# A kernel whose ring of small buffers is moved down by 480 bytes in SBUF

## The chip, the cores and the metric

The kernel runs on one core of a Trainium2 chip. The metric is device time in microseconds (us), the median of the runs shown; lower is better. One more execution was recorded by the hardware profiler, and all rows below come from that one.

## What is computed

Three stages in a row, all in float32. First attention over 4 batches and 8 heads of 768 positions with 64 elements per head: each query sees the 31 keys within 15 positions of it, and one summary (maximum of keys, mean of values) of each block of 32 positions. Its output is read as 3,072 tokens of 512 elements. Second, a wide layer; third, a mixture of 8 experts with 4 slots each:

```python
# wide layer, x is [3072, 512], w_in [512, 2048], w_out [2048, 512]
h = x @ w_in
g = h * np.cos(h)
x2 = g @ w_out
# mixture
logits = x2 @ phi                      # [3072, 32]
d = softmax(logits, axis=0); slot_input = d.T @ x2
slot_out = [np.maximum(slot_input[e] @ w1[e], 0) @ w2[e] for e in range(8)]
out = softmax(logits, axis=1) @ slot_out
```

## The kernel before, in words

**The wide layer.** The tokens are taken in six batches of 512. In each batch the inner width of 2,048 is taken in 16 slots of 128, so there are 96 slots. To keep float32 accuracy with single-pass matmuls, each operand is split into a rounded high part and a remainder (fp32r tiles): the tokens into `xh` and `xl` (lines 536 and 540), a slot's weights into `wih`, `wil`, `woh`, `wol` (lines 553 and 560), the slot's result `g` into `gh` and `gl` (lines 622 and 631). A product then takes three matmuls: high by high, high by remainder, remainder by high.

**The first product** of a slot (`mm1_hi`, `mm1_lo`; lines 580, 581, 588) is 12 matmuls into one PSUM bank, each with 128x128 stationary weights and a moving operand of 512 columns:

```python
nc.tensor.matmul(h, hi[:, c], xh[s // NF][:, t, :], start=t == 0, stop=False)   # 580
nc.tensor.matmul(h, hi[:, c], xl[s // NF][:, t, :], start=False, stop=False)    # 581
nc.tensor.matmul(h, lo[:, c], xh[s // NF][:, t, :], start=False, stop=t == 3)   # 588
```

The stationary operand (second argument) is a slice of 128 columns, 512 bytes, of `wih` or `wil`; the moving one is a whole row of 2,048 bytes of `xh` or `xl`.

**The second product** (`mm2_hi`, `mm2_lo`; lines 666, 667, 675) is 12 matmuls into four banks, the stationary operand a slice of `gh` or `gl`, the moving one the whole of `woh` or `wol`:

```python
nc.tensor.matmul(acc[t], gh[:, c], hi, start=f == 0, stop=False)                # 666
nc.tensor.matmul(acc[t], gh[:, c], lo, start=False, stop=False)                 # 667
nc.tensor.matmul(acc[t], gl[:, c], hi, start=False, stop=f == NF - 1)           # 675
```

In the last batch (`mm2_last`; lines 652, 653, 655) the two change places: `woh` and `wol` are stationary, `gh` and `gl` move. In every stream of these matmuls each one needs weights of its own to be loaded, and the load for the next one runs beside the current one.

**Between the matmuls** of a slot, VectorE and ScalarE compute `g` (lines 600, 604, 608, 618), ScalarE rounds (lines 553, 622) and GpSimd takes the remainders (lines 560, 631). Between slots stand pieces of attention for later batches (scores L382, transposes L467, values L502) and of the mixture (transposes L712, logits L726, sums L837). After the last batch the experts run (L1172, L1218) and the outputs are combined (L1253); their weights `ex` come by DMA into buffers as these are released.

**Order.** The order on every engine up to slot 80 is written out by name in a long string (`ORDER`), the rest follows the order of the code. Addresses play no part in it.

**Places in SBUF.** Pools are laid from address 0 upward, those with `side="right"` from the upper end downward. The pool `ring` holds the eleven small kinds of tile named above except `xh` and `xl`; every one of them is 2,048 bytes per partition, so all of them begin at the same remainder by 2,048. `xh` and `xl` lie in the pool `xres`; their rows are 2,048 bytes too. In the built kernel:

| tiles | pool | address in a partition | remainder by 2,048 |
|---|---|---|---|
| `xh`, `xl` (rows of 2,048 bytes) | xres | 69,120 to 101,888 | 1,536 |
| `gh`, `gl` | ring | 196,576 to 208,864 | 2,016 |
| `wih`, `woh`, `wol` | ring | 208,864 to 221,152 | 2,016 |
| `a`, `wil` | ring | 221,152 to 229,344 | 2,016 |
| weights `w` as loaded | wres | 3,584 to 69,120 | 1,536 |

When the wide layer is done, the pool `tail` takes the place of `ring`: seven tiles of expert weights (`ex`), which later hold four of the twelve output tiles, and one tile `cT0`. Ten tiles of the first attention batches (`aT`) lie in the ring as well.

Of the kernel before, what the change touches and what calls it, by code (L numbers as in the profile page):

```python
# [10 lines left out]
F32 = mybir.dt.float32  # L11
# [60 lines left out]
def body(ctx: ExitStack, tc: tile.TileContext, q0, qk, kT, vT, vn, vx, w, phi, ex, cst, out):  # L72
# [7 lines left out]
    ps_acc = ctx.enter_context(tc.tile_pool(name="ps_acc", bufs=1, space=PSUM))  # L80
    ps_h = ctx.enter_context(tc.tile_pool(name="ps_h", bufs=2, space=PSUM))
    ps_m = ctx.enter_context(tc.tile_pool(name="ps_m", bufs=2, space=PSUM))
    ring_cm = tc.tile_pool(name="ring", bufs=2, side="right", reuse_waits="tile")
    ring = ring_cm.__enter__()
    att_cm = tc.tile_pool(name="att", bufs=2, reuse_waits="tile")
# [1265 lines left out]
```

## Time and profile before

| | |
|---|---|
| median of 3 runs | 719.12 us (718.82 to 720.0) |
| profiled execution, its own time | 720.67 us |
| its span, first to last instruction | 718.9 us |
| TensorE (PE) busy | 701.7 us, 98% of the span |
| PE's weight loads (PEld), beside the matmuls | 545.8 us |
| VectorE (DVE) / ScalarE (ACT) / GpSimd (POOL) busy | 440.9 / 409.7 / 412.5 us |
| mean granted clock of TensorE | 0.996 |

The span holds nearly all of the profiled execution's time (1.8 us lie around it). Matmuls overlap: the record of one runs on while the next has begun, so the distance from one start to the next tells what a matmul costs, and the length of its record does not.

### The profile page before, as it was taken

What the parts mean: (1) busy time and instruction counts of PE and PEld (TensorE: products, weight loads), DVE (VectorE), ACT (ScalarE), POOL (GpSimd) and SP (SyncE); (2) the same over time, 40 slices, a digit from 0 to 9 for tenths busy, and PEclk for the clock granted to TensorE, in tenths of its full rate; (3) what the DMA queues carried; (4) which work ended last, traced back from release to release, by engine and by line L of the source; (5) the groups of instructions that cost most, each with busy time, mean ns of one, the idle gap of its engine ahead of it and who ended that gap; (6) DMA issues with size and microseconds to landing.
All of it is one profiled execution on the core that took longest, in us unless ns stands there. A gap on an engine that the chain in (4) does not pass through costs nothing.

```text
span 718.9 us, 12964 instructions
## 1 busy us (share of the span) xinstructions
PE 701.7 (98%) x5092; PEld 545.8 (76%) x5092; DVE 440.9 (61%) x680; ACT 409.7 (57%) x772; POOL 412.5 (57%) x310
## 2 busy tenths in 40 slices
PE   8999999999999999999999999999999999999994
PEld 6678777888787788878887787887787887787453
DVE  6799988784665856855756765665763335434323
ACT  5999997563754654744654844644745446434122
POOL 1776867765566564665754675754667665752000
PEclk9999999999999999999999999999999999999998
DMA  9998866210413302202102203101002922327998
GB/s 334 421 345 288 317 207 245 77 58 0 133 36 139 105 1 78 98 0 105 53 1 72 83 1 107 46 1 46 28 1 84 407 105 79 116 89 273 409 375 291
DMA packets 34861, 101.64 MB, mean 141 GB/s; under 512 B 3440, under 2 KB 13936, under 8 KB 32752
## 3 DMA queue, kind: packets, MB, share of 16 engines
q1 hardware_dynamic: 34800, 100.81, 38.4%
q8 instruction: 40, 0.66, 0.4%
q14 instruction: 21, 0.17, 0.1%
HBM read 92.54 MB, written 6.29 MB: 137 GB/s over the span
## 4 chain that ended last, share of the span: by engine, by line
PE 89%; DMA 4%; ACT 3%; DVE 1%; issue 1%; SPq 0%; DVEq 0%
PE h L580 13%; PE h L581 12%; PE h L588 12%; PE acc L666 10%; PE acc L675 10%; PE acc L667 10%; DMA raw<-in_w_dram 4%; PE av L502 3%; PE sc L382 2%; PE tr L467 2%; PE acc L652 2%; PE acc L653 2%; PE acc L655 2%; PE yp L1218 2%; PE hp L1172 2%; PE xt L712 1%
## 5 line engine op out<-in xcount | busy, mean ns | idle before, releaser
L631 POOL TENSOR_TENSOR gl<-a,gh 128x512 fp32r<-128x512 f32 x96 | 131.0, 1366 | 115.2 <-ACT gh L622 70.0
L560 POOL TENSOR_TENSOR wol<-w,woh 128x512 fp32r<-128x512 f32 x96 | 127.7, 1333 | 82.3 <-ACT woh L553 75.7
L580 PE MATMUL h<-xh,wih 128*128 128x512 f32 x384 | 155.3, 404 | 2.3 <-DVE a L618 1.4
L581 PE MATMUL h<-xl,wih 128*128 128x512 f32 x384 | 151.9, 395 | 0.2 <-DVE xl L540 0.2
L600 DVE TENSOR_SCALAR a<-h 128x512 f32<-128x512 f32 x96 | 66.0, 687 | 126.0 <-PE h L588 84.9
L608 ACT ACTIVATE a<-a,halfpi 128x512 f32<-128x512 f32 x96 | 69.4, 723 | 105.1 <-DVE a L604 104.7
L666 PE MATMUL acc<-woh,gh 128*128 128x512 f32 x320 | 127.3, 398 | 0.0
L667 PE MATMUL acc<-wol,gh 128*128 128x512 f32 x320 | 125.4, 392 | 0.0
L560 POOL TENSOR_TENSOR wil<-w,wih 128x512 fp32r<-128x512 f32 x81 | 108.5, 1345 | 16.9 <-ACT wih L553 8.9
L588 PE MATMUL h<-xh,wil 128*128 128x512 f32 x384 | 105.1, 398 | 0.0
L618 DVE TENSOR_TENSOR a<-h,a 128x512 f32<-128x512 f32 x96 | 65.7, 687 | 43.3 <-ACT a L608 43.0
L580 PEld LDWEIGHTS h<-xh,wih 128*128 128x128 f32 x384 | 72.1, 188 | 22.6 <-DVE a L618 2.3
L675 PE MATMUL acc<-woh,gl 128*128 128x512 f32 x320 | 88.3, 397 | 0.0
L588 PEld LDWEIGHTS h<-xh,wil 128*128 128x128 f32 x384 | 71.0, 188 | 17.6 <-POOL wol L560 0.8
L581 PEld LDWEIGHTS h<-xl,wih 128*128 128x128 f32 x384 | 72.1, 188 | 16.0 <-DVE xl L540 0.5
L553 ACT CAST woh<-w 128x512 fp32r<-128x512 f32 x96 | 59.4, 619 | 40.3 <-PE acc L675 34.3
L553 ACT CAST wih<-w 128x512 fp32r<-128x512 f32 x96 | 59.1, 619 | 28.5 <-PE h L581 18.4
L622 ACT CAST gh<-a 128x512 fp32r<-128x512 f32 x96 | 58.9, 616 | 26.8 <-PE acc L667 19.2
L666 PEld LDWEIGHTS acc<-woh,gh 128*128 128x128 f32 x320 | 60.1, 188 | 14.8 <-issue 1.5
L667 PEld LDWEIGHTS acc<-wol,gh 128*128 128x128 f32 x320 | 60.2, 188 | 12.9
L675 PEld LDWEIGHTS acc<-woh,gl 128*128 128x128 f32 x320 | 58.7, 188 | 12.8 <-issue 0.3
L604 DVE SCALAR_TENSOR_TENSOR a<-a,h 128x512 f32<-128x512 f32 x96 | 65.5, 683 | 2.3
(155 smaller groups left out, 946.6 us busy)
## 6 DMA issues: line engine op xcount, KB each, us to landing
ex<-in_ex_dram SPq DMA_DIRECT2D x64, 512.0 KB
raw<-in_w_dram SPq DMA_DIRECT2D x16, 1024.0 KB
qk<-in_qk_dram SPq DMA_DIRECT2D x20, 736.0 KB
v<-in_vx_dram SPq DMA_DIRECT2D x24, 512.0 KB
kr<-in_kT_dram SPq DMA_DIRECT2D x16, 384.0 KB
out_dram<-o SPq DMA_DIRECT2D x12, 512.0 KB
vr<-in_vT_dram SPq DMA_DIRECT2D x12, 384.0 KB
v<-vs SPq DMA_DIRECT2D x40, 48.0 KB
```

Source lines behind the costliest of these rows:

```text
L553: nc.scalar.copy(hi, W[f][:, part, :])
L560: (eng or nc.gpsimd).tensor_tensor(out=lo, in0=W[f][:, part, :], in1=hi, op=ALU.subtract)
L580: nc.tensor.matmul(h, hi[:, c], xh[s // NF][:, t, :], start=t == 0, stop=False)
L581: nc.tensor.matmul(h, hi[:, c], xl[s // NF][:, t, :], start=False, stop=False)
L588: nc.tensor.matmul(h, lo[:, c], xh[s // NF][:, t, :], start=False, stop=t == 3)
L600: nc.vector.tensor_scalar(out=a, in0=h, scalar1=0.25, scalar2=MAGIC, op0=ALU.add, op1=ALU.add)
L608: turn_dve["sin"] = nc.scalar.activation(a, a, AF.Sin, bias=halfpi, scale=-TWO_PI)
L618: nc.vector.tensor_tensor(out=a, in0=h, in1=a, op=ALU.mult)
L631: nc.gpsimd.tensor_tensor(out=gl, in0=a, in1=gh, op=ALU.subtract)
L666: nc.tensor.matmul(acc[t], gh[:, c], hi, start=f == 0, stop=False)
L667: nc.tensor.matmul(acc[t], gh[:, c], lo, start=False, stop=False)
L675: nc.tensor.matmul(acc[t], gl[:, c], hi, start=False, stop=f == NF - 1)
```

## The change

One line is added, ahead of the pool `ring`. It reserves a tile of 120 float32 elements, 480 bytes per partition, at the upper end of SBUF. Nothing reads or writes it. No instruction is added, removed or moved on any engine.

```diff
     ps_m = ctx.enter_context(tc.tile_pool(name="ps_m", bufs=2, space=PSUM))
+    ctx.enter_context(tc.tile_pool(name="edge", bufs=1, side="right")).tile([128, 120], F32, name="edge")
     ring_cm = tc.tile_pool(name="ring", bufs=2, side="right", reuse_waits="tile")
```

All tiles of `ring`, and later of `tail`, lie 480 bytes lower: `gh` at 196,096 in place of 196,576, and so on, with remainder 1,536 in place of 2,016. All other tiles stay where they were.

## Rows read from the trace of the kernel before

**Rows 1.** Windows: busy us (instructions) of each engine, granted clock, DMA.
```profile
34.00:100.00 66.00, 63.86 (x446) 49.76 (x445) 60.03 (x88) 64.32 (x143) 46.17 (x27) 1.00 0.81 294
100.00:200.00 100.00, 100.00 (x697) 80.28 (x696) 72.48 (x103) 62.74 (x102) 67.67 (x49) 1.00 0.35 120
...
400.00:500.00 100.00, 99.57 (x638) 79.33 (x630) 62.62 (x93) 54.49 (x93) 62.42 (x50) 1.00 0.15 49
500.00:600.00 100.00, 100.00 (x616) 80.04 (x615) 50.71 (x83) 50.79 (x88) 66.77 (x52) 1.00 0.32 123
600.00:659.00 59.00, 59.00 (x263) 46.56 (x265) 23.97 (x39) 28.68 (x48) 35.04 (x28) 1.00 0.35 122
659.00:719.00 60.00, 48.84 (x551) 28.12 (x551) 20.30 (x46) 15.57 (x33) 0.73 (x1) 0.95 0.95 354
```

**Rows 2.** Waits, whole span: engine and line <- releaser: us, times, longest.
```profile
DVE a L600 <- PE h L588: 84.9, 40, 5.1
...
ACT woh L553 <- PE acc L675: 34.3, 24, 5.2
...
PE h L580 <- DVE a L618: 1.4, 2, 1.0
```

**Rows 3.** PE timeline, 139 to 150 us: start, length, line, operation, count.
```profile
139.49 2.03 PE L588 MATMUL h<-xh,wil 128*128 128x512 f32 x8
141.36 1.09 PE L675 MATMUL acc<-woh,gl 128*128 128x512 f32 x4
142.29 0.39 PE L666 MATMUL acc<-woh,gh 128*128 128x512 f32 x1
...
144.12 1.07 PE L675 MATMUL acc<-woh,gl 128*128 128x512 f32 x4
145.02 0.39 PE L666 MATMUL acc<-woh,gh 128*128 128x512 f32 x1
...
146.84 0.40 PE L580 MATMUL h<-xh,wih 128*128 128x512 f32 x1
...
149.64 0.39 PE L580 MATMUL h<-xh,wih 128*128 128x512 f32 x1
```

**Rows 4.** Lengths of the matmuls' records, whole span: minimum, median, maximum in ns.
```profile
L588 PE MATMUL h<-xh,wil x384: 388/396/505, 36.9 to 650.3; 128*128 128x512 f32 x192
L675 PE MATMUL acc<-woh,gl x320: 387/390/504, 52.6 to 570.9; 128*128 128x512 f32 x160
L655 PE MATMUL acc<-gl,woh x64: 389/389/434, 575.7 to 658.6; 128*128 128x512 f32 x64
```

**Rows 5.** Groups of PE, 100 to 659 us: line, shape, count; busy us, mean ns.
```profile
L580 PE MATMUL h<-xh,wih 128*128 128x512 f32 x340 | 137.0, 403 | 0.4 <-DVE a L618 0.4
L581 PE MATMUL h<-xl,wih 128*128 128x512 f32 x340 | 134.4, 395 | 0.0
L666 PE MATMUL acc<-woh,gh 128*128 128x512 f32 x288 | 114.6, 398 | 0.0
...
L588 PE MATMUL h<-xh,wil 128*128 128x512 f32 x343 | 94.1, 398 | 0.0
...
L652 PE MATMUL acc<-gh,woh 128*128 128x512 f32 x64 | 25.5, 399 | 0.0
```

**Rows 6.** Groups of PE over the whole span: the work between the streams.
```profile
L467 PE MATMUL tr<-ident,S 128*120 128x128 f32 x192 | 27.8, 275 | 0.1
...
L502 PE MATMUL av<-aT,v 120*64 120x64 f32 x640 | 23.0, 225 | 0.0
L382 PE MATMUL sc<-qk 64*64 64x120 f32 x640 | 21.0, 269 | 0.0
...
L712 PE MATMUL xt<-ident,x 128*128 128x128 f32 x80 | 11.7, 274 | 0.0
```

**Rows 7.** Two lines of GpSimd: minimum, median, maximum ns of one.
```profile
L631 POOL TENSOR_TENSOR gl<-a,gh x96: 1270/1297/2167, 45.0 to 655.5; 128x512 fp32r<-128x512 f32 x96
```
```profile
L560 POOL TENSOR_TENSOR wol<-w,woh x96: 1267/1295/2225, 28.7 to 654.3; 128x512 fp32r<-128x512 f32 x96
```

**Rows 8.** Experts' matmuls: moving tiles outside the ring, then inside: minimum, median, maximum ns.
```profile
L1218 PE MATMUL yp<-ex,hT x32: 379/379/379, 683.4 to 684.9; 128*32 128x256 f32 x32
```
```profile
L1218 PE MATMUL yp<-ex,hT x32: 379/379/379, 685.1 to 686.6; 128*32 128x256 f32 x32
```

## The prediction

> **What bounds the kernel now.** I read the windows by stage first. [...] Then the waits: VectorE waits 84.9 us in all for line 588 and ScalarE 34.3 us for line 675, while the longest entry of TensorE itself is 1.4 us in two waits [rows 2]. So in the wide layer the others wait for TensorE, and TensorE for nobody. What a matmul costs there, from its start to the next one's, is what the time is made of. Between 34 and 100 us it is less clear: ScalarE is busy for 64.32 of 66 us and TensorE for 63.86, so either may set the pace. After 659 us the experts run, with the DMA engines at a share of 0.95.
>
> Then the PE timeline, where the reader is to take differences of starts [rows 3]. Twelve matmuls of the first product, from 146.84 to 149.64 us, take 2.80 us: 233.3 ns each. Eight of line 588, from 139.49 to 141.36, take 1.87: 234 ns. The first twelve of the second product behind them, to 144.12, take 2.76: 230 ns. The next twelve, to 146.84, take 2.72: 226.7 ns. So there are two levels, although all are 128x128 by 128x512 in the same type, at the same clock. The second product begins high and settles at 226.7 ns; the first stays at about 233.3. This is no matter of one stretch: the median record of line 588 is 396 ns long, of line 675 390, and of line 655 in the last batch 389 [rows 4]; where matmuls follow each other closely, the record's length moves with the distance.
>
> What differs between the two? Not the shape, nor the reuse of weights: lines 580 and 581 load one slice twice and move two tiles, and so do 666 and 667. Not the bank of the output: 666 and 667 write one bank twice, line 675 a new one each time, and both are among the twelve at 226.7. Not the slice of the weights: both products step through a tile by 512 bytes. Not which tile stands still: in the last batch `wo` and `g` change places, and line 655 still has the low level. What is left is where the operands lie. In the second product both begin at remainder 2,016 by 2,048. In the first the moving rows begin at 1,536 and the weights at 2,016; by 512, to which the slices step, that is a difference of 32 bytes against none. Also, `xh` and `xl` lie far below the ring. The trace holds these differences only together, so which of them matters can't be read from it.
>
> **The change part by part.** *What it adds in work:* nothing. Every engine has the same instructions in the same order with the same waits, and the reserved tile is never touched: 0 us.
>
> *The first product.* After the change the moving rows and the weights both begin at 1,536, a difference of none, as the second product has it now. If the difference is what costs, these matmuls fall to 226.7 ns once settled. From 100 to 659 us there are 340 + 340 + 343 = 1,023 of them [rows 5], at 233.3 - 226.7 = 6.6 ns: 6.75 us.
>
> *The second product.* Both operands move together, so their difference stays none. Its first dozen behind the first product costs 230 and not 226.7 [rows 3]. If that is the rest of another rhythm, it goes when the first product has the same one. There are 3 x 288 + 3 x 64 = 1,056 [rows 5], nearly all within a dozen of such a switch: 3.3 ns each, 3.5 us.
>
> *What stays.* The streams are interrupted, and I assume that each new beginning costs a dozen at 230: 12 x 3.3 = 0.04 us. The pieces between: 192/4 = 48 blocks of transposes, 640/32 = 20 of values and 20 of scores, 80/4 = 20 of the mixture's transposes [rows 6], 108 in all, some before 100 us: about 100, or 4.0 us.
>
> *Sum:* 6.75 + 3.5 - 4.0 = 6.2 us. Its ends: if the first product only comes to the 230 that the second has behind a switch, and the second gains nothing, 1,023 x 3.3 = 3.4 us. If no beginning costs anything, 10.2 us. I take 6.2 because the rows show both the settled level and the dozen before it.
>
> *Stage 34 to 100 us:* I count nothing, with ScalarE busy for 97% of it [rows 1]; if TensorE sets the pace there, the other 129 and 96 matmuls would give 1.2 us more.
>
> *The other engines' reads and writes of the ring.* GpSimd's line 631 has all three operands at 2,016 and a median of 1,297 ns; line 560 reads one at 1,536 and has 1,295 [rows 7]. Equal remainders cost no more than 2 ns there, so I price the move at 0; the 96 instructions of each line at 2 ns would be 0.4 us on an engine that is busy for two thirds of the time.
>
> *What is late next.* A slot of about 7 us would shorten by 0.08 us, and VectorE alone waits nearly 0.9 us a slot for line 588 [rows 2]. So TensorE stays the bound. If that cover failed, the gain would be lost slot by slot, down to nothing.
>
> *The experts' stage.* Their weights are loaded as buffers come free, which TensorE paces; before 659 us the DMA share is 0.35 [rows 1], so loads that start earlier meet no crowd, and the stage moves forward whole. Without that, only the last batch's part, 59 of 559 us, would be lost: 0.7 us. Seven weight tiles, four output tiles and `cT0` also move; their matmuls are in the part that I price at 0 (below).
>
> **The profiled execution against the median.** It took 720.67 us, above all three runs, of which the median is 719.12. With 6.2 us less its span would be 712.7 and its own time 714.5; the median becomes 719.12 - 6.2 = 712.9 us.
>
> **Rivals.**
>
> *Nothing changes: 719.1 us.* The two levels may come from where the tiles lie in the large, 69 to 102 thousand against 197 and more, or from something that I haven't named; 480 bytes don't touch that. For it: in the experts' matmuls, moving tiles outside the ring at 1,536 and tiles in it at 2,016 give records of 379 ns alike [rows 8], and GpSimd doesn't care either. Against it: those matmuls load only 32 columns of weights, so little is read beside the moving operand, and the two levels are there all the same in the streams. [...]
>
> *Slower: 722.6 us.* The start of the moving operand decides alone: at 1,536 a stream doesn't settle, at 2,016 it does. Then the first product stays as it is, and the second, whose `woh` and `wol` now begin at 1,536, loses its low level: 1,056 x (233.3 - 230) = 3.5 us. For it: in the streams, 1,536 goes with the high level and 2,016 with the low one without exception. Against it: [rows 8] show no such effect of the moving start alone, and an even start of both operands is no evident handicap. It decides if 666, 667 and 675 no longer come to 226.7.
>
> *A part of the gain: 715.7 us.* The first product comes to 230 only, as in the lower end above. This is within the forecast's own range.
>
> **How the numbers follow.** The forecast (both products settle) has 0.57, with its own range of 708.5 (the 10.2 us and a little of the early stage) to 715.7. No change has 0.27, the slower rival 0.16. About 0.2%, 1.4 us, is what a measurement of this kernel can tell from no change. So faster 0.57, same 0.27, slower 0.16. The range from 708.5 to 720.4 takes in the forecast and no change, and leaves out the slower rival.
>
> **What the changed profile would show.** Right: in the PE timeline twelve matmuls of lines 580 and 581 (one line further down in the new file) in 2.72 to 2.76 us and not 2.80, the median record of line 588 at about 390 ns and not 396, the first dozen of the second product behind the first at 2.72; TensorE still busy all through the wide layer; GpSimd's medians within a few ns of 1,295. If lines 580, 581 and 588 still step by 233.3, the first term was wrong; if 666, 667 and 675 rise to 233, the slower rival holds; if the steps fall and the time doesn't, the cover of the other engines was too thin.

## The result, and the profile after

The changed kernel takes **712.1 us** (median of four runs, 711.56 to 712.95), against 719.56 us (718.82 to 720.1) for the kernel before on the same chip: a ratio of 0.9898, with a 95% interval of 0.9883 to 0.9913. The prediction was 712.9 us, "faster" with a chance of 0.57, and a range of 708.5 to 720.4. The profiled execution took 712.95 us with a span of 711.2; before, it was 720.67 with 718.9. So the spans differ by 7.7 us, the medians by 7.5.

The PE timeline of the changed kernel, at the place of [rows 3] (start us, length us, engine, line, operation, count; every line below the inserted one stands one further down, so 580, 581, 588, 666, 667, 675 are now 581, 582, 589, 667, 668, 676):

```profile
138.09 1.98 PE L589 MATMUL h<-xh,wil 128*128 128x512 f32 x8
139.90 1.07 PE L676 MATMUL acc<-woh,gl 128*128 128x512 f32 x4
...
142.62 1.07 PE L676 MATMUL acc<-woh,gl 128*128 128x512 f32 x4
...
145.34 0.39 PE L581 MATMUL h<-xh,wih 128*128 128x512 f32 x1
...
148.06 0.39 PE L581 MATMUL h<-xh,wih 128*128 128x512 f32 x1
```

Take the differences of the starts. Eight of line 589: 138.09 to 139.90, 1.81 us and no longer 1.87. The dozen of the second product behind them: 2.72 and no longer 2.76. The next dozen 2.72, as before. The dozen of the first product, 145.34 to 148.06: 2.72 and no longer 2.80. All of them now step by about 226.7 ns. The work is the same, instruction for instruction.

The lengths of the records answer [rows 4] (minimum, median, maximum in ns):

```profile
L589 PE MATMUL h<-xh,wil x384: 387/389/504, 37.3 to 642.6; 128*128 128x512 f32 x192
...
L676 PE MATMUL acc<-woh,gl x320: 388/389/504, 53.0 to 564.6; 128*128 128x512 f32 x160
...
L656 PE MATMUL acc<-gl,woh x64: 388/389/441, 569.3 to 650.9; 128*128 128x512 f32 x64
```

The median of line 588 was 396; as line 589 it is 389, that of all the others. The windows answer [rows 1] (stretch and its length, then busy us and instructions of PE, its weight loads, DVE, ACT and POOL, granted clock, DMA share, GB/s):

```profile
34.00:100.00 66.00, 64.58 (x460) 51.05 (x457) 60.08 (x88) 65.78 (x145) 47.03 (x28) 1.00 0.80 293
100.00:200.00 100.00, 100.00 (x702) 81.21 (x701) 73.14 (x105) 62.76 (x103) 67.78 (x49) 1.00 0.34 121
...
500.00:600.00 100.00, 100.00 (x569) 81.44 (x567) 52.06 (x87) 52.49 (x93) 69.28 (x54) 1.00 0.31 118
...
652.00:712.00 60.00, 48.12 (x531) 27.54 (x527) 20.27 (x45) 14.98 (x32) 0.73 (x1) 0.95 0.93 352
```

TensorE is still busy through the wide layer at the same granted clock of 1.00. What became shorter is the time from one start to the next, not idle time. The busy times show this badly, since a stretch that was full stays full. The last window is placed 7 us earlier than its counterpart, and its numbers are nearly the same: the experts' stage came forward whole. And the waits, which answer [rows 2] (us in all, times, longest):

```profile
DVE a L601 <- PE h L589: 85.9, 43, 5.0
...
ACT woh L554 <- PE acc L676: 33.2, 24, 5.2
...
PE h L581 <- DVE a L619: 1.8, 3, 1.1
```

VectorE and ScalarE still wait for TensorE, nearly as long as before; TensorE's own longest entry went from 1.4 to 1.8 us. The bound has not moved.

A timeline shows one place. For the whole span I worked out, from the starts of all matmuls in each trace, the mean distance from each matmul of a product to the next matmul of the wide layer, where that follows directly and less than 300 ns later (some 1,050 such distances in the first product and 1,060 in the second). It went from 233.2 to 228.4 ns in the first product and from 229.9 to 228.0 in the second. Each product has 1,152 matmuls: 1,152 x 4.8 = 5.5 us and 1,152 x 1.9 = 2.2 us, 7.7 together if every matmul is counted. That this is just the difference of the spans is in part luck: 0.9 us of that difference is there by 100 us already, where the two traces differ in their clock too (see "The early stage" below). The account from 100 us on is the one to trust: 6.8 us.

### The profile page after: what moved, and what is told of

The parts are those of the page before. It is cut to its first block, busy times and chain, and to the rows that moved or that the text cites. A ratio compares the mean times of both kernels' runs of the same rounds, so it can differ in the third digit from the quotient of the medians.

```text
span 711.2 us, 12964 instructions
## 1 busy us (share of the span) xinstructions
PE 694.8 (98%) x5092; PEld 547.2 (77%) x5092; DVE 440.1 (62%) x680; ACT 409.6 (58%) x772; POOL 411.9 (58%) x310
## 4 chain that ended last, share of the span: by engine, by line
PE 90%; DVE 4%; ACT 3%; issue 1%; DVEq 0%
PE h L581 12%; PE h L582 12%; PE h L589 12%; PE acc L667 10%; PE acc L676 10%; PE acc L668 10%; PE tr L468 3%; PE av L503 3%; PE sc L383 2%; PE acc L653 2%; PE acc L656 2%; PE acc L654 2%; PE yp L1219 2%; PE hp L1173 2%; PE xt L713 1%; PE sp L838 1%
## 5 line engine op out<-in xcount | busy, mean ns | idle before, releaser
L581 PE MATMUL h<-xh,wih 128*128 128x512 f32 x384 | 153.5, 400 | 1.8 <-DVE a L619 1.8
L582 PE MATMUL h<-xl,wih 128*128 128x512 f32 x384 | 150.2, 391 | 0.1
L589 PE MATMUL h<-xh,wil 128*128 128x512 f32 x384 | 103.2, 394 | 0.0
```

## The experiments

The change moves one thing and thereby several: the ring's absolute start, its start against that of `xh` and `xl`, the ring's place, and the bytes left free. My theory was that the *difference* between the start of the moving operand and that of the weights decides. In what follows "difference" is the start of the moving operand minus that of the weights, reduced to 0 to 255 by taking away multiples of 256 (that 256 is the right number came out only in the course of the runs). Before, it was 32 in the first product (1,536 - 2,016 = -480) and 0 in the second. All experiments that change the tile `edge` alone keep the second product's difference at 0.

**Experiment 1: a ring moved by 32 bytes only.** The changed kernel, with 32 free bytes and not 480, which makes the difference 64:

```diff
-    ....tile([128, 120], F32, name="edge")
+    ....tile([128, 8], F32, name="edge")
```

> The ring lies 32 bytes lower than before, not 480: its tiles begin at 1,984 by 2,048, xh and xl stay at 1,536. The difference of moving and stationary starts is then none by 64 bytes, but 64 by 512 and 448 by 2,048. Theory A (the difference by 64 sets the step of a matmul): both products settle at 226.7 ns, the whole gain of the change, median about 712. Theory B (the difference counts by 512 or by 2,048): the first product stays near 233.3 ns, the median at 717 to 719.5.

Measured: 716.47 us, ratio 0.9957 (0.994 to 0.9974); mean distances 230.5 and 229.8 ns in the first and the second product. This is a part of the gain, and neither theory had it. The PE timeline of this run, at the same place:

```profile
145.36 0.40 PE L581 MATMUL h<-xh,wih 128*128 128x512 f32 x1
...
148.12 0.39 PE L581 MATMUL h<-xh,wih 128*128 128x512 f32 x1
```

The dozen takes 2.76 us, between 2.72 and 2.80. So the pattern is not one of equal or unequal remainder by 64: a difference of 64 is better than 32 and worse than 0.

**Experiment 2: move the other operand.** The kernel before, but with 480 free bytes at the lower end, ahead of the pool of `xh` and `xl`. Now `xh` and `xl` begin at 2,016 as well, where the tiles of the ring have always begun:

```diff
+    ctx.enter_context(tc.tile_pool(name="edge", bufs=1)).tile([128, 120], F32, name="edge")
```

> The ring stays where it was (2,016) and the 480 bytes are left free below xh and xl, which then begin at 2,016 too; the tiles between them and the ring move up with them. Differences are none, but every start lies 32 bytes off a multiple of 64. Theory A (only the difference counts): both products settle at 226.7 ns, median about 712. Theory C (starts at a multiple of 64 are what is good): no gain, 719, or, if 2,016 is bad for a moving operand, slower.

Measured: 712.2 us, ratio 0.99 (0.9883 to 0.9918); 228.4 and 228.0 ns, the numbers of the changed kernel. Its PE timeline:

```profile
139.66 1.07 PE L676 MATMUL acc<-woh,gl 128*128 128x512 f32 x4
...
142.38 1.07 PE L676 MATMUL acc<-woh,gl 128*128 128x512 f32 x4
...
145.10 0.39 PE L581 MATMUL h<-xh,wih 128*128 128x512 f32 x1
...
147.82 0.39 PE L581 MATMUL h<-xh,wih 128*128 128x512 f32 x1
```

Each dozen takes 2.72 us. So the ring's absolute start doesn't matter, nor does its place: here it lies where it lay before (the tiles between `xl` and the ring are 480 bytes higher). What is common to this kernel and the changed one is the equal start.

**Experiment 3: nearly as many free bytes, but no equal start.** 448 bytes, which puts the ring at 1,568 and the difference at 224 (-32):

```diff
-    ....tile([128, 120], F32, name="edge")
+    ....tile([128, 112], F32, name="edge")
```

> The ring lies 448 bytes lower than before, its tiles begin at 1,568 by 2,048, nearly where the change puts them, but 32 bytes off xh and xl again. Theory A and theory C: the first product steps by 233 ns as before, the second by 228 to 230, median about 719. If the free space or the rough place of the ring brings the gain: about 712.

Measured: 718.64 us, ratio 0.9994 (0.9972 to 1.0015); 233.2 and 229.0 ns. Its PE timeline:

```profile
145.78 0.40 PE L581 MATMUL h<-xh,wih 128*128 128x512 f32 x1
...
148.58 0.40 PE L581 MATMUL h<-xh,wih 128*128 128x512 f32 x1
```

The dozen takes 2.80 us, as before the change. No gain is shown, though the ring was moved nearly as far. The first product has the same 233.2 as before, 32 bytes on the other side.

**Experiment 4: equal starts in the first product, 32 bytes apart in the second.** The changed kernel, with a small tile in the ring behind one of the buffers, which puts `gh` and `gl` at 1,504 while `wih`, `wil`, `woh` and `wol` stay at 1,536:

```diff
         aT = pool.tile([KC, 512], F32, name=f"aT{g}_{j}", tag=tag, bufs=n)
+        if g == 2 and j == 1:
+            ring.tile([128, 8], F32, name="gap", tag="gap", bufs=1)
```

> The changed kernel with 32 bytes more, between gh, gl and the other tiles of the ring: gh and gl begin at 1,504, the rest at 1,536. The first product keeps equal starts, the second (stationary gh or gl, moving woh or wol) is set 32 bytes apart. Theory A: the first product stays at 227 to 228 ns, the second goes from 228.0 to 233, 1,152 x 5.2 ns = 6.0 us, and the first begins out of step behind it: median 717 to 719. A theory in which the moving start alone counts (woh, wol, xh, xl are all at 1,536 as in the changed kernel): 712.

Measured: 717.56 us, ratio 0.9979 (0.9968 to 0.9989). The first product is at 229.0 ns, the second at 232.9. Its PE timeline (here the lines are two further down again, 583, 591, 669, 678):

```profile
137.88 1.98 PE L591 MATMUL h<-xh,wil 128*128 128x512 f32 x8
139.71 1.09 PE L678 MATMUL acc<-woh,gl 128*128 128x512 f32 x4
...
142.50 1.09 PE L678 MATMUL acc<-woh,gl 128*128 128x512 f32 x4
...
145.30 0.39 PE L583 MATMUL h<-xh,wih 128*128 128x512 f32 x1
...
148.02 0.39 PE L583 MATMUL h<-xh,wih 128*128 128x512 f32 x1
```

The two products have changed roles: the dozens of the second take 2.79 and 2.80 us, that of the first 2.72. The records agree (minimum, median, maximum in ns):

```profile
L591 PE MATMUL h<-xh,wil x384: 387/389/504, 36.6 to 647.3; 128*128 128x512 f32 x192
...
L678 PE MATMUL acc<-woh,gl x320: 388/394/502, 52.3 to 568.1; 128*128 128x512 f32 x160
```

So nothing about the first product itself (its tiles' place, its outputs, its order) gave it the high level; the same level can be given to the second. It also speaks against the rival by which the moving start alone decides: in the second product of this kernel, the moving `woh` and `wol` of batches before the last begin at 1,536, as `woh` and `wol` do in the changed kernel, and yet the level is the high one.

**Experiments 5 to 7: how far the pattern repeats.** The first run had left open which number the difference is to be taken by. Three paddings: 96 bytes (difference 128), 224 (-256, so 0 by 256, but not by 512 or 2,048) and 992 (512, so 0 by 512, but not by 2,048):

```diff
-    ....tile([128, 120], F32, name="edge")
+    ....tile([128, 24], F32, name="edge")     # experiment 5
+    ....tile([128, 56], F32, name="edge")     # experiment 6
+    ....tile([128, 248], F32, name="edge")    # experiment 7
```

> The ring begins at 1,920 by 2,048, xh and xl at 1,536: a difference of 128 by 512 in the first product, none in the second. With 32 bytes apart the first product steps by 233.2 ns, with 64 by 230.5, with none by 228.4. Theory A1 (the pattern repeats every 128 bytes): 228.4 ns and a median of 712. Theory A2 (it repeats every 256 or 512 bytes only): the first product between 229 and 234 ns, a median of 714 to 719.

> The ring begins at 1,792 by 2,048: a difference of 256 by 512 in the first product, none in the second. Theory A1 (repeats every 128) and a pattern of 256: 228.4 ns, a median of 712. A pattern of 512: between 229 and 234 ns, 714 to 719.

> The ring begins at 1,024 by 2,048, 512 away from xh and xl, so the starts agree by 512 and not by 2,048, the remainder that the change names. Since the weights are slices that step by 512 bytes, every form of the theory of differences says that this is as good as the change: 228.4 ns in both products, a median of 712. If the remainder by 2,048 or by 1,024 counts: 714 to 719.

Measured: with 96 bytes 717.79 us, ratio 0.9973 (0.9953 to 0.9993), 232.4 and 229.1 ns; with 224 bytes 713.14 us, 0.9899 (0.9865 to 0.9933), 228.55 and 228.05 ns; with 992 bytes 711.81 us, 0.9887 (0.9837 to 0.9937), 228.3 and 228.0 ns. The records of line 589 in the run with 96, the one with 224 and the one with 992:

```profile
L589 PE MATMUL h<-xh,wil x384: 387/393/505, 36.6 to 647.1; 128*128 128x512 f32 x192
```
```profile
L589 PE MATMUL h<-xh,wil x384: 387/389/628, 37.5 to 643.1; 128*128 128x512 f32 x192
```
```profile
L589 PE MATMUL h<-xh,wil x384: 387/389/504, 35.6 to 640.9; 128*128 128x512 f32 x192
```

Differences of -256, 0 and 512 give the whole gain, 128 gives little of it. So it is enough that the two starts agree by 256 bytes; the 2,048 in the change's description is more than is needed, and any of 224, 480 and 992 free bytes would have done. The intervals of the four versions with equal starts overlap, so none of them is shown to be better than the change.

**Experiments 8 to 10: the points between.** 64, 128 and 160 free bytes, differences of 96, 160 and 192:

```diff
-    ....tile([128, 120], F32, name="edge")
+    ....tile([128, 16], F32, name="edge")     # experiment 8
+    ....tile([128, 32], F32, name="edge")     # experiment 9
+    ....tile([128, 40], F32, name="edge")     # experiment 10
```

> Difference of 96 by 256 in the first product, none in the second. So far by 256: none 228.4 to 228.6 ns, 32 and 224 both 233.2, 64 230.5, 128 232.4. If only none is good: 230 to 234 ns, a span of 714 to 719. If some other difference settles lower than 226.7, the first product falls below 228 and the span below 710.

> Difference of 160 by 256 in the first product, none in the second. If only none is good: 230 to 234 ns, a span of 714 to 719. If the pattern is even about none, as 32 and 224 suggest, it is like the difference of 96.

> Difference of 192 by 256 in the first product, none in the second. If only none is good: 230 to 234 ns, a span of 714 to 719. If the pattern is even about none, it is like the difference of 64: 230.5 ns, a span near 715.

Measured: 720.86, 717.8 and 718.32 us (single times, without an interval), beside 719.97 for the kernel before, also a single time. So here the distances count and not the times. The records of line 589 in these three runs (their median was 389 ns with the change and, as line 588, 396 without it):

```profile
L589 PE MATMUL h<-xh,wil x384: 388/396/503, 37.5 to 650.5; 128*128 128x512 f32 x192
```
```profile
L589 PE MATMUL h<-xh,wil x384: 389/394/505, 35.7 to 647.4; 128*128 128x512 f32 x192
```
```profile
L589 PE MATMUL h<-xh,wil x384: 390/394/502, 36.3 to 648.0; 128*128 128x512 f32 x192
```

All runs together, by the difference in the first product:

| difference by 256 | kernel | first product, ns | second product, ns | span, us |
|---|---|---|---|---|
| 0 | the change | 228.4 | 228.0 | 711.2 |
| 0 | 2: all at 2,016 | 228.4 | 228.0 | 711.0 |
| 0 | 6: 224 bytes | 228.55 | 228.05 | 711.6 |
| 0 | 7: 992 bytes | 228.3 | 228.0 | 709.4 |
| 32 | before | 233.2 | 229.9 | 718.9 |
| 64 | 1: 32 bytes | 230.5 | 229.8 | 714.9 |
| 96 | 8: 64 bytes | 234.0 | 229.9 | 719.1 |
| 128 | 5: 96 bytes | 232.4 | 229.1 | 715.7 |
| 160 | 9: 128 bytes | 233.7 | 228.9 | 716.0 |
| 192 | 10: 160 bytes | 233.3 | 229.2 | 716.5 |
| 224 | 3: 448 bytes | 233.2 | 229.0 | 717.1 |
| 0 (second product: 32, in the last batch 224) | 4: gap | 229.0 | 232.9 | 716.0 |

Only 0 comes to the low level. 64 lies half way. The pattern isn't quite even about 0: 32 and 224 are alike, 96 and 160 nearly so, but 64 gives 230.5 and 192, as far on the other side, 233.3. One of my expectations had these two alike, and they are not.

A mean mixes the distances just behind a switch from one product to the other with those that come later. I parted them, after 100 us. The first product steps, from the fifth distance behind a switch on, by 226.9 ns with the change, 228.8 at a difference of 64, 233.9 at 128, and 233.1 to 234.4 at the others. So the 232.4 of 128 is no better level: only its first four distances are shorter, 231.2 ns.

The second product, whose starts are always equal but in experiment 4, moves too, between 228.0 and 229.9. Its first four distances behind a switch are 232.1 ns in the kernel before and 227.4 with the change; from the ninth on they are 227.1 in both. So it is what the first product leaves behind at each switch that moves it.

## Why the prediction was right

**The first step**, the reading of two levels at one clock and the exclusion of everything but the operands' starts, held. Experiments 2 and 4 show what the trace of before could not tell apart, the difference and not the place or the absolute start.

**The first product.** Predicted: 1,023 matmuls after 100 us by 6.6 ns, 6.75 us. In the means it is 233.2 - 228.4 = 4.85 ns (unrounded), 5.0 us. The 6.6 ns was the settled level against the high one, and the part that does not settle was taken off separately, as the restarts.

**The second product.** Predicted: 1,056 by 3.3 ns, 3.5 us, before the restarts are taken off. Measured: 229.9 - 228.0 = 1.84 ns (unrounded), 1.9 us. The mechanism is the predicted one: the first dozen behind a switch went from 2.76 to 2.72 us, and over the whole trace it is the distances just behind a switch that fell.

**The restarts.** Predicted: 4.0 us stay. By the means, what is still above the settled level is (228.4 - 226.7) x 1,023 + (228.0 - 226.7) x 1,056 = 3.1 us. The PE timeline of the changed kernel shows one such beginning in the last batch, behind transposes (line 713), and, further on, eight matmuls with a long uninterrupted stream ahead of them:

```profile
576.56 0.60 PE L713 MATMUL xt<-ident,x 128*128 128x128 f32 x4
576.92 0.48 PE L581 MATMUL h<-xh,wih 128*128 128x512 f32 x1
577.23 0.39 PE L582 MATMUL h<-xl,wih 128*128 128x512 f32 x1
...
579.99 0.39 PE L654 MATMUL acc<-gh,wol 128*128 128x512 f32 x1
...
588.42 0.39 PE L581 MATMUL h<-xh,wih 128*128 128x512 f32 x1
...
590.23 1.07 PE L589 MATMUL h<-xh,wil 128*128 128x512 f32 x4
```

From 577.23 to 579.99, twelve matmuls from the second behind the interruption on, it is 2.76 us, 230 ns each, as assumed. The eight from 588.42 to 590.23 take 1.81 us, 226 ns each. The rest of the trace agrees. Sorted by their place behind such a beginning (the first distance, of over 300 ns, left out), the distances of the changed kernel after 100 us are 233.3 ns from the second to the fourth, 229.3 from the fifth to the eleventh, and 226.8 from the twelfth on; in the kernel before, those from the twelfth on are still 231.4. So equal starts do not give the low level at once, and the term belonged in the sum. It was sized 0.9 us too large: both traces have 80 such beginnings after 100 us, not 100, and 80 x 0.04 would have been 3.2.

**The sum.** Predicted 6.2 us after 100 us; by the means, carried over to every matmul, it is 5.0 + 1.9 = 6.9, and by the start times of the same matmuls in both traces, from 100 to 658.6 us, 6.8. So this stretch gave 0.6 us more than predicted. The medians differ by 7.5 us, 1.3 more than the sum. What is left of that lies ahead of 100 us or between executions; the runs do not part the two. That 712.1 is only 0.8 below the 712.9 comes from the kernel before, whose median was 719.56 beside it and 719.12 in the runs I started from.

**The early stage** was counted at 0, at most 1.2 us. Against the trace of before, the same matmuls start 0.98 us later at 34 us and 0.92 us earlier at 100. A part of this is the clock: at 25 us the changed kernel was 0.24 us earlier, at 31 us 0.98 later, and in between its granted clock fell. The windows up to 34 us, before and then after:

```profile
0.00:34.00 34.00, 30.47 (x504) 22.37 (x504) 23.30 (x44) 24.36 (x82) 14.90 (x17) 1.00 0.96 375
```
```profile
0.00:34.00 34.00, 30.54 (x496) 23.26 (x498) 23.40 (x44) 24.22 (x81) 15.07 (x17) 0.95 0.97 378
```

The 0.95 comes from one stretch, 27.0 to 30.4 us, in which the granted clock was 0.50. TensorE had been busy for 23.5 of the 27 us ahead of it, and for 23.6 in the trace of before, where the clock did not fall there. Experiment 8, which gains nothing, has such a stretch too: its matmuls start 1.17 us later than before at 34 us and 0.40 earlier at 100. Experiment 3, which gains nothing in the first product, has none: 0.79 earlier and 1.02 earlier. So most of this varies from execution to execution, and what the change is worth there can't be told from these traces.

**The cover and the experts.** No engine took TensorE's place, as the waits above show; the lead grows evenly (1.6 us at 150, 3.2 at 300, 5.4 at 500, 7.7 at 658.6) and stays at 7.7 to 705 us: the experts' loads did not give it back.

**GpSimd.** Priced at 0; the medians were 1,297 and 1,295 ns [rows 7]:

```profile
L632 POOL TENSOR_TENSOR gl<-a,gh x96: 1268/1295/2155, 45.4 to 647.8; 128x512 fp32r<-128x512 f32 x96
```
```profile
L561 POOL TENSOR_TENSOR wol<-w,woh x96: 1272/1292/2227, 27.6 to 646.5; 128x512 fp32r<-128x512 f32 x96
```

**The rivals.** "Nothing changes" falls with the result: the addresses alone move the mean step of the first product from 228.4 ns (the change) to as much as 234.0 (experiment 8). "Slower" falls too: `woh` and `wol` moving at 1,536 came to 2.72 us a dozen in the changed kernel. "A part of the gain" (715.7) was not this change, but 32 free bytes come near it (716.47, with the first product at 230.5).

One thing the argument could not have carried: it knew two points, a difference of none and one of 32, and nothing between or beyond. For a change that made the difference 64 or 128 it would have had to promise the whole gain or none, and experiments 1 and 5 gave a part.

## What to carry to other kernels

Where TensorE bounds a stretch of back-to-back matmuls, each with a load of its own weights, take the distances of their starts: two levels at one shape, type and clock, here 226.7 and 233.3 ns, are worth an explanation. For matmuls of this shape and type (no other was tried), lay moving and stationary tiles so that their starts agree by 256 bytes: here the first product then stepped by 228.3 to 229.0 ns in the mean, and at every other difference tried by 230.5 to 234.0. A few hundred bytes of padding at one end of the memory were enough (224, 480 or 992), and it didn't matter which of the two was moved (712.1 and 712.2 us). Count only what settles: streams that are interrupted often keep a part of the loss, here 3.1 of 10 us (behind an interruption 233.3 ns from the second distance to the fourth, 226.8 from the twelfth on).

## What the runs showed of the hardware

I had not expected that the pattern repeats by 256 bytes and not by 64 or 2,048, nor that it has a half-way point at 64 (230.5 ns) with nothing like it at 192 (233.3). It is shown to repeat for the difference of 0 alone (228.55 ns at -256, 228.4 at 0, 228.3 at 512); whether 32 and 288 are alike wasn't tried, nor any difference finer than 32 bytes. That a stream carries its rhythm over into the next one stood in the prediction as an "if", and the runs bear it out: the second product, with equal starts throughout, stepped by 229.8 to 229.9 ns in the mean beside a first product at 32, 64 or 96, by 228.9 to 229.2 beside one at 128 to 224, and by 228.0 beside one at 0.

What in the chip makes this is open. The runs show at which differences the step is short and at which it is long, and no cause. The experts' matmuls of [rows 8], whose loads are a quarter as wide (32 columns of weights against 128), show no level: 379 ns at either start of the moving tile. No run here tells whether the current matmul's weights or the next one's are concerned, or whether another type than this one behaves in the same way.
